# Two small opening tiles share one second stage, and the later softmax is spread over the run

## The chip, the cores and the metric

The kernel runs on one core of a Trainium2 chip. The core has five engines that run their own instruction queues: TensorE (PE, matmuls, with weight loads shown apart as PEld), VectorE (DVE), ScalarE (ACT), GpSimd (POOL) and SyncE (SP, which only issues DMAs here). The metric is the device time of one execution in microseconds; smaller is better.

## The reference

Three layers on `x` of 2 x 4160 tokens x 192 channels. Cut to what matters:

```python
# 1 attention: each token is a softmax-weighted sum of its last 7 tokens
w = softmax(weight_gen, axis=-1)                   # (2, 4160, 8 heads, 7)
out = einsum('bshk,bskhg->bshg', w, x_unf)         # 24 channels per head
# 2 first mix: a blend with the token before, then two matmuls and a gate
xk = mu_k * x + (1 - mu_k) * x_prev
xr = mu_r * x + (1 - mu_r) * x_prev
v = np.maximum(xk @ w_k, 0)**2 @ w_v               # 192 -> 1024 -> 192
x = sigmoid(xr @ w_r) * v
# 3 second mix: two matmuls with a 3-tap convolution over tokens between them
h = np.maximum(x @ w_in, 0)                        # 192 -> 1024
conv = conv_w[0]*h[t-1] + conv_w[1]*h[t] + conv_w[2]*h[t+1]
return (h * sigmoid(conv)) @ w_out                 # 1024 -> 192
```

## The kernel before

The 4160 tokens of each of the two batches are cut into ten tiles (`SIZES`: 256, 248, seven of 472, 352), and one loop runs over the tiles. The work of one tile has four parts.

`attention` runs on POOL. A tile has 2, 3 or 4 slots per batch; one slot of one batch (128 partitions, one token each) is a **token group**: a product of `rows` and `sw` (1344 elements per partition), two folding sums into `prod` and a last sum into `tok`. The weights `sw` come from `softmax`: a maximum and a subtraction, an Exp on ACT, a sum and a reciprocal on DVE, and a product on POOL. `softmax_load` 3 brings the weights of tiles 3 to 9 in one DMA.

`mixing` makes the input of the first mix. Three **flips** per tile (unit `u` 0, 2 and 1) transpose tokens on PE into a `pa` bank; ACT and DVE blend each with its shifted copy, and `hi` and `lo` split the result into two parts, `xA` for the first 128 channels and, for unit 2, `xB` for the other 64 of both batches, which DMAs put in place. Unit 2 needs all the token groups of the tile.

`moe1` is the first mix, in eight **slices** of 128 hidden channels for each batch: five matmuls into a `pa` bank (three read `xA`, two `xB`), Relu, Square and a rounded copy `s` on ACT, a remainder on DVE, and five matmuls into the banks `am` and `ar`. `gate_r` adds two gates per batch through the same two `pa` banks. `mix_out` multiplies by the gate and writes the tile `x2` of the batch.

`moe2` is the second mix, again in eight slices per batch: five matmuls from `x2` into one of two `pc` banks, then `h` (Relu), a scaled copy, two taps (`tap`, DVE), a Sigmoid, a product and the split `g`, and five matmuls into `bm` and `br`. `store` sends these out. `LAG` puts it ten steps behind `moe1`.

The weights are also split by ACT and DVE on the chip, piece by piece (`prepare`). Every call is planned at a time in steps with `at`; `Program.schedule` then takes the calls through costs of its own and writes out a fixed order for each engine. So each engine's order is settled before the run, and an instruction that waits holds up all behind it on its engine.

In the rows every call has the same line (169, after: 173), since one place issues all of them; tiles are told apart by name and width: 256 is tile 0, 248 tile 1, 472 a full tile (250, 258 and 474 where two halo columns are added).

Of the kernel before, what the change touches and what calls it, by code (L numbers as in the profile page):

```python
# [8 lines left out]
F32R = mybir.dt.float32r  # L9
# [22 lines left out]
def f(ap):  # L32
    return ap.bitcast(F32)


class Program:
# [37 lines left out]
    def cost(self, eng, method, out, ins, pointer):  # L74

        n = self.count(out)
        src = [self.space(x) for x in ins]
        if method == "dma_start":
            return 0.6, 0.0
        if eng == "PE":  # L80
            busy = max(n * 0.00045 + 0.002, 0.109)
            return busy, busy + 0.24
        if eng == "ACT":
            near = bool(src) and src[0] == "PSUM"
            p = 0.1 if pointer else 0.0
            return (0.06 if near else 0.09) + p + n / 1200, (0.2 if near else 0.24) + p + n / 1200
        if eng == "DVE":
            if method == "tensor_reduce":
                n = self.count(ins[0])
            if method == "reciprocal":  # L90
                return 0.07 + n / 160, 0.2 + n / 160
            if method in ("tensor_scalar", "tensor_copy", "memset") and "PSUM" not in src:
                return 0.07 + n / 1920, 0.2 + n / 1920
            stt = method == "scalar_tensor_tensor"
            return (0.13 if stt else 0.07) + n / 960, (0.26 if stt else 0.2) + n / 960
        if eng == "POOL":
            busy = 0.1 + (n / 455 if method == "tensor_tensor" else n / 270)
            return busy, busy + 0.12
        return 0.6, 0.6

    def schedule(self):
# [42 lines left out]
        for _ in range(n):  # L144
# [39 lines left out]
def conv_moe_kernel(ctx: ExitStack, tc: tile.TileContext, xp, wg_first, wg_rest, mus, w_k, w_v, w_r, w_in, conv_w, w_out, out):  # L184
# [210 lines left out]
    def softmax(j, a, b, eng, times, bank):  # L395
# [19 lines left out]
        for t, fn in zip(times, (lambda: fold(m, ALU.max), lambda: each(m, ALU.subtract), s3,  # L415
                                 lambda: fold(z, ALU.add), s5, lambda: each(m, ALU.mult))):
            at(t, fn)

# [35 lines left out]
    def mixing(i, u, t, dt_):  # L454
        N, P, e = SIZES[i], PART[i], EXTRA[i]
        c = 1 if u == 2 else 0
        st = {}

        def flip():
            p = pa_r()  # L460
            st["p"] = p[:, e:e + N]
            st["q"] = p
            x = tok_t[i]
            k = (0, 256, 128)[u]
            for l in range(SLOTS[i]):
                PE.transpose(p[:, l:l + SLOTS[i] * (P - 1) + 1:SLOTS[i]], x[:, l, k:k + 128], ident)

        def shifted(fn):
            a = att_r()[:, :N]
            if e:  # L470
                fn(a, st["q"][:, e - 1:e + N - 1])
            else:
                POOL.memset(a[:, 0:1], 0.0)
                fn(a[:, 1:N], st["q"][:, 0:N - 1])
            return a
# [5 lines left out]
        def m1(k):  # L481
            st[k] = (am_r, ar_r)[k]() if i == 0 else mk_r()
            col = 2 * k + c
            own = slice(col, col + 1)
            if i < 2:
                a = shifted(lambda y, x: ACT.activation(y, x, ACTF.Copy, scale=onemu[:, own]))
                DVE.scalar_tensor_tensor(out=st[k][:, :N], in0=st["p"], scalar=mu[:, own], in1=a, op0=ALU.mult, op1=ALU.add)
            else:
                DVE.scalar_tensor_tensor(out=st[k][:, :N], in0=st["d"], scalar=onemu[:, own],
                                         in1=st["p"], op0=ALU.mult, op1=ALU.add)  # L490

        def hi(k):
            if u < 2:
                x = xA_r[k]()
                xin[i, u, k, 0] = x
            else:
                x = rm_r[k]().unsqueeze(1)
            st["h", k] = x
            ACT.copy(x[:, 0, :N], st[k][:, :N])

        def lo(k):
            x = st["h", k]
            y = x[:, 1, :N] if u < 2 else (mk_r() if i == 0 else st[k])[:, :N].bitcast(F32R)
            (POOL if i else DVE).tensor_tensor(y, st[k][:, :N], f(x[:, 0, :N]), op=ALU.subtract)
            if u == 2:
                for b in range(NB):
# [5 lines left out]
                    SP.dma_start(out=f(z[oth, :N]), in_=f(y[own]))  # L512

# [249 lines left out]
    mixing(0, 1, -70, 0.1)  # L763

    for i in range(NTILE):
        T = 16 * i
        if i:
            for b in range(NB):
                attention(i, b, T - 22 + 4.5 * b, T - 15 + 4.5 * b, 1.125, POOL, (25.0 + 8 * b if i == 1 else 0.0, 0.0))
            for u, t in ((0, T - 5), (2, T - 3.7), (1, T + 3)) if i > 1 else ((0, 7), (2, 8.3), (1, 15)):  # L770
                mixing(i, u, t, 2.5)
        for b in range(NB):
# [8 lines left out]
            store(i, b, t + LAG + 10.02)  # L781

# [68 lines left out]
```

## Time and profile before

| | |
|---|---|
| median of 3 runs | 779.31 us (778.96 to 781.27) |
| time of the profiled execution | 780.29 us |
| its span, first to last instruction | 778.5 us |
| busy: PE, ACT, DVE, POOL | 694.1, 665.5, 630.8, 506.6 us |
| mean granted clock of TensorE | 0.974 |

The profiled execution's own time is 1.8 us over its span, and 1.0 us over the median. The clock is given as a share of 2.4 GHz, so 0.50 is the lower level of 1.2 GHz. Busy times of matmuls are modelled, and neighbours overlap: how fast matmuls follow each other is read from their starts.

### The profile page before, as it was taken

To read this page: it belongs to the slowest core of one execution; us is meant where nothing else is said; L and a number is where in the kernel's file an instruction comes from. 1 tells how busy PE (TensorE), PEld (TensorE's weight loads), DVE (VectorE), ACT (ScalarE), POOL (GpSimd) and SP (SyncE) were. 2 spreads that over 40 slices of the span, in tenths; PEclk is the share of its full clock that TensorE was granted. 3 is DMA by queue.
4 is the path that set the end of the run, shared out by engine and by line. 5 is a ranking of instruction groups with operands and counts; after the bars stand their busy time and mean duration, and the time that the engine had idled before them with its cause. 6 is when DMAs were issued, how large, how long until landed. Compare 5 with 4: busy or idle time off the path is not lost.

```text
span 778.5 us, 10782 instructions
## 1 busy us (share of the span) xinstructions
PE 694.1 (89%) x3505; PEld 606.3 (78%) x3505; DVE 630.8 (81%) x1137; ACT 665.5 (85%) x1441; POOL 506.6 (65%) x368
## 2 busy tenths in 40 slices
PE   0065776999999999999999999999999999999985
PEld 0054676898888888888888888888888888888974
DVE  6997977886878787878787888788788878788886
ACT  2466797998989898989998989898989899999985
POOL 6998888899999999999999798565702010110000
PEclk9996886999999999999999999999999999999999
DMA  7685010130130112111221120120002000200000
GB/s 224 197 269 180 4 52 11 58 105 11 62 101 18 53 70 51 70 51 52 69 70 51 39 78 20 45 63 7 20 0 70 1 19 1 57 0 19 19 2 28
DMA packets 19240, 45.09 MB, mean 58 GB/s; under 512 B 3056, under 2 KB 14704, under 8 KB 19056
## 3 DMA queue, kind: packets, MB, share of 16 engines
q1 hardware_dynamic: 19184, 44.41, 18.9%
q8 instruction: 27, 0.44, 0.2%
q14 instruction: 29, 0.24, 0.1%
HBM read 27.40 MB, written 6.39 MB: 43 GB/s over the span
## 4 chain that ended last, share of the span: by engine, by line
PE 68%; ACT 14%; DVE 14%; issue 2%; DMA 1%; SPq 0%; ACTq 0%; DVEq 0%
PE pa L169 21%; PE pc L169 16%; PE am L169 10%; PE bm L169 9%; PE ar L169 7%; PE br L169 6%; DVE pc L169 4%; ACT pa L169 2%; DVE stage L169 2%; ACT pc L169 2%; ACT h L169 2%; ACT g L169 2%; ACT L169 1%; DVE bm L169 1%; DVE s L169 1%
## 5 line engine op out<-in xcount | busy, mean ns | idle before, releaser
L169 DVE SCALAR_TENSOR_TENSOR pc<-h,cw,pc 128x472 f32<-128x472 f32 (+3 forms) x312 | 203.7, 653 | 34.9 <-ACT pc L169 31.9
L169 POOL TENSOR_TENSOR prod<-rows,sw 128x1344 f32<-128x1344 f32 x70 | 216.1, 3087 | 11.0 <-DMA rows<-in_x_dram 6.0
L169 ACT ACTIVATE pa<-pa 128x472 f32<-128x472 f32 (+3 forms) x324 | 162.7, 504 | 37.9 <-PE pa L169 33.8
L169 POOL TENSOR_TENSOR prod<-prod 128x576 f32<-128x576 f32 (+1 forms) x140 | 171.2, 1223 | 8.6
L169 PE MATMUL am<-s,wv 128*128 128x472 f32 (+3 forms) x480 | 146.9, 366 | 7.5 <-ACT s L169 6.0
L169 PE MATMUL bm<-g,wo 128*128 128x472 f32 (+3 forms) x465 | 144.5, 361 | 9.6 <-ACT g L169 9.0
L169 DVE TENSOR_TENSOR pc<-h,pc 128x472 f32<-128x472 f32 (+3 forms) x156 | 92.6, 594 | 54.4 <-ACT pc L169 53.0
L169 PE MATMUL pa<-xA,wkA 128*128 128x472 f32 (+3 forms) x480 | 124.4, 363 | 7.5 <-DVE s L169 3.5
L169 PE MATMUL pc<-x,wiA 128*128 128x474 f32 (+3 forms) x468 | 118.6, 361 | 3.2 <-DVE g L169 3.2
L169 POOL TENSOR_TENSOR xA<-mk,xA 128x472 fp32r<-128x472 f32 (+2 forms) x36 | 40.5, 1130 | 122.1 <-ACT xA L169 95.8
L169 PE MATMUL ar<-s,wv 128*128 128x472 f32 (+3 forms) x320 | 112.0, 362 | 5.0 <-DVE x L169 3.3
L169 PE MATMUL br<-g,wo 128*128 128x472 f32 (+3 forms) x310 | 109.4, 356 | 0.0
L169 DVE TENSOR_TENSOR s<-pa,s 128x472 fp32r<-128x472 f32 (+3 forms) x162 | 94.9, 586 | 16.0 <-ACT s L169 15.0
L169 PEld LDWEIGHTS am<-s,wv 128*128 128x128 f32 x480 | 88.7, 196 | 22.4 <-ACT s L169 11.2
L169 DVE TENSOR_TENSOR g<-pc,g 128x472 fp32r<-128x472 f32 (+3 forms) x153 | 90.4, 591 | 16.4 <-ACT g L169 14.9
L169 PEld LDWEIGHTS bm<-g,wo 128*128 128x128 f32 x465 | 86.5, 192 | 21.1 <-ACT g L169 11.5
L169 PEld LDWEIGHTS pa<-xA,wkA 128*128 128x128 f32 x480 | 86.4, 196 | 19.8 <-DVE s L169 6.3
L169 ACT ACTIVATE pc<-h,cw 128x472 f32<-128x472 f32 (+3 forms) x156 | 97.5, 625 | 1.6
L169 PEld LDWEIGHTS pc<-x,wiA 128*128 128x128 f32 x468 | 84.3, 194 | 14.0 <-DVE g L169 4.5
L169 ACT ACTIVATE h<-pc 128x474 f32<-128x474 f32 (+3 forms) x156 | 82.5, 529 | 9.6 <-PE pc L169 7.5
L169 PE MATMUL pa<-xB,wkB 128*128 128x472 f32 (+3 forms) x320 | 89.0, 359 | 1.1 <-DMA xB<-mk 1.1
L169 PE MATMUL pc<-x,wiB 128*128 128x474 f32 (+3 forms) x312 | 87.4, 359 | 0.0
(121 smaller groups left out, 1086.9 us busy)
## 6 DMA issues: line engine op xcount, KB each, us to landing
rows<-in_x_dram SPq DMA_DIRECT2D x14, 960.0 KB, 4.5
xB<-rm SPq DMA_DIRECT2D x28, 118.0 KB, 2.3
xB<-mk SPq DMA_DIRECT2D x28, 118.0 KB, 2.3
out_dram<-om SPq DMA_DIRECT2D x14, 236.0 KB, 2.0
rows<-in_x_dram SPq DMA_DIRECT2D x4, 768.0 KB, 6.6
rows<-in_x_dram SPq DMA_DIRECT2D x2, 864.0 KB, 4.3
out_dram<-ob SPq DMA_DIRECT2D x14, 118.0 KB, 2.2
stage<-in_moe_w_v_dram SPq DMA_DIRECT2D x4, 384.0 KB, 3.8
```

Of the source, the lines that this page charges most:

```text
L169: getattr(self.real[eng], method)(*a, **k)
```

## The change

- The second mix takes tiles 0 and 1 as one: `moe2` and `store` run only from tile 1 on, with 476 columns there (`UNIT`); both tiles write into the same `x2`, side by side (`OFFSET`). So there are nine second stages per batch, where there were ten.
- The tiles become 256, 220, seven of 476, and 352.
- Of the softmax of tiles 3 to 9, only the maximum and the subtraction stay close together. Tile 3 has its Exp alone; tiles 4 to 9 share one Exp over 2576 columns; the sum, the reciprocal and the last product of each tile come 16 steps apart.
- The pieces of the second mix's weights are planned at wider times. The softmax products of tiles 1 and 2 move behind the tokens of tile 0, the first `rows` load goes ahead of the first weights, and six clearings on POOL become two on DVE.
- Flips go through their slots in the other order. Unit kinds 3 and 4 are added in the code but used by no tile.
- In `schedule`: other costs for a reduction and for POOL, no delay from POOL to POOL, and `ins` no longer drops an operand that is also written.

```diff
-SIZES = [256, 248] + [472] * 7 + [352]
+SIZES = [256, 220] + [476] * 7 + [352]
+OFFSET = [0, SIZES[0]] + [0] * (NTILE - 2)
+UNIT = [None, SIZES[0] + SIZES[1]] + SIZES[2:]
...
-            busy = 0.1 + (n / 455 if method == "tensor_tensor" else n / 270)
-            return busy, busy + 0.12
+            busy = 0.15 + (n / 455 if method == "tensor_tensor" else n / 270)
+            return busy, busy + 0.1
...
-            ins = [x for x in aps if x is not out]
+            ins = [x for x in [*a[0 if "out" in k else 1:], *(v for key, v in k.items() if key != "out")]
...
-            for l in range(SLOTS[i]):
+            for l in reversed(range(SLOTS[i])):
...
-        c = slice(2, N + 2)
+        c = slice(OFFSET[i] + 2, OFFSET[i] + N + 2)
...
-        N = SIZES[i] + (2 if last else 0)
+        N = UNIT[i] + (2 if last else 0)
...
-        softmax(3, a, b, POOL, (16.5 + 0.3 * j, 16.6 + 0.3 * j, 19.5 + 0.1 * j, 20.5 + 0.5 * j, 20.6 + 0.5 * j, 24.9 + 16 * j), None)
+        softmax(3, a, b, POOL, (30.3, 30.4, 31.2, 32.0, 32.1, 34.9) if j == 0 else
+                (36.9 + 1.2 * j, 37 + 1.2 * j, None, 30 + 16 * j, 30.1 + 16 * j, 32.5 + 16 * j), None)
+    a = slots[3]
+    at(45.3, lambda: ACT.activation(sm[3][0][:, a:], sm[3][0][:, a:], ACTF.Exp))
...
-                moe2(i, b, fi, t + fi + LAG)
+                if i:
+                    moe2(i, b, fi, t + fi + LAG)
```

How the orders move, at three places.

POOL, before, among the token groups of tile 2 (`tok_79`; `sw<-sw,stage` are steps of the softmax of tiles 3 to 9):

```order
TENSOR_TENSOR prod<-prod 128x384
TENSOR_TENSOR sw<-sw,stage 128x448 x2
TENSOR_TENSOR tok_79<-prod 128x192
TENSOR_TENSOR sw<-sw,stage 128x448 x4
TENSOR_TENSOR sw<-sw,stage 128x336
TENSOR_TENSOR prod<-rows_76,sw 128x1344
TENSOR_TENSOR sw<-sw,stage 128x448
```

POOL, after, from the last token group of tile 2 on:

```order
TENSOR_TENSOR prod<-rows_77,sw 128x1344
TENSOR_TENSOR prod<-prod 128x576
TENSOR_TENSOR prod<-prod 128x384
TENSOR_TENSOR tok_79<-prod 128x192
TENSOR_TENSOR xA_87<-mk_83,xA_87 128x476
TENSOR_TENSOR xA_89<-mk_84,xA_89 128x476
TENSOR_TENSOR sw<-sw,stage 128x448 x2
TENSOR_TENSOR mk_83<-mk_83,rm_85 128x476
TENSOR_TENSOR sw<-sw,stage 128x448 x2
TENSOR_TENSOR mk_84<-mk_84,rm_86 128x476
TENSOR_TENSOR sw<-sw,stage 128x448
```

All fourteen such steps stood ahead of tile 2's last token group; now none does, and five stand between it and tile 3's first.

ACT, before, at one of the Exps of the later softmax (there are seven, among slices of the first two tiles):

```order
ACTIVATE pa_111<-pa_111 128x256 x2
ACT_TABLE_LOAD
ACTIVATE sw<-sw 128x448
ACT_TABLE_LOAD
ACTIVATE pc_113<-pc_113 128x256
```

ACT, after, at the one Exp of tiles 4 to 9, which stands among slices of tile 2:

```order
ACTIVATE h_103<-pc_113 128x478
ACT_TABLE_LOAD
ACTIVATE sw<-sw 128x2576
ACTIVATE pc_113<-h_103,cw 128x476
ACTIVATE pa_111<-pa_111 128x476
CAST rm_85<-mk_83 128x476
ACT_TABLE_LOAD
ACTIVATE r_97<-pa_112 128x476
```

Fourteen table loads become six: two early ones, two around tile 3's Exp and these two.

PE, before, where the first matmul of tile 2 stands (`pa_111<-xA_87,wkA`, 472 wide); `pc` rows are second stages of tile 1:

```order
MATMUL pc_113<-x_0_73,wiA 128x250 x3
MATMUL pc_113<-x_0_73,wiB 128x250 x2
MATMUL bm<-g_101,wo 128x248 x2
MATMUL br<-g_101,wo 128x248
MATMUL bm<-g_101,wo 128x248
MATMUL br<-g_101,wo 128x248
MATMUL am<-s_99,wv 128x248 x2
MATMUL ar<-s_99,wv 128x248
MATMUL pa_111<-xA_87,wkA 128x472
```

PE, after, at the same place, from the flip of tile 2's unit 2 on:

```order
MATMUL pa_111<-ident,tok_79 128x128 x4
MATMUL pc_114<-x_0_73,wiA 128x478 x3
MATMUL pc_114<-x_0_73,wiB 128x478 x2
MATMUL bm<-g_102,wo 128x476
MATMUL br<-g_102,wo 128x476
MATMUL am<-s_100,wv 128x220 x2
MATMUL ar<-s_100,wv 128x220
MATMUL am<-s_100,wv 128x220
MATMUL ar<-s_100,wv 128x220
MATMUL pa_112<-xA_87,wkA 128x476 x3
```

Before, all 16 slices of tile 0's second stage and five of tile 1's stand ahead of this matmul; now six of the joint second stage do, and ten are left.

## Rows read from the trace of the kernel before

**Rows 1.** The page: span, and busy time (share) and instructions by engine
```profile
span 778.5 us, 10782 instructions
PE 694.1 (89%) x3505; PEld 606.3 (78%) x3505; DVE 630.8 (81%) x1137; ACT 665.5 (85%) x1441; POOL 506.6 (65%) x368
```

**Rows 2.** Stretches: busy us (x instructions) by engine, granted clock, DMA
```profile
40.00:60.00 20.00, 13.96 (x75) 12.00 (x75) 18.04 (x40) 14.96 (x43) 19.05 (x16) 1.00 0.90 268
...
66.00:82.00 16.00, 9.91 (x41) 9.06 (x42) 14.94 (x34) 10.28 (x29) 15.53 (x12) 0.50 0.24 65
...
82.00:94.00 12.00, 8.87 (x63) 7.52 (x61) 11.59 (x23) 10.71 (x26) 9.10 (x10) 1.00 0.00 1
...
240.00:680.00 440.00, 437.37 (x2060) 377.95 (x2059) 357.58 (x579) 400.34 (x801) 290.56 (x200) 1.00 0.14 43
```

**Rows 3.** Timeline of PE, where tile 2 begins: start us, us, instruction
```profile
40.27 0.98 PE L169 MATMUL pa<-xA,wkA 128*128 128x256 f32 x3 [2.33 <-ACT rm L169]
...
150.89 0.52 PE L169 MATMUL pc<-x,wiA 128*128 128x250 f32 x3
...
152.07 0.40 PE L169 MATMUL pa<-xA,wkA 128*128 128x248 f32 x2
...
154.55 0.63 PE L169 MATMUL pa<-ident,tok 128*128 128x128 f32 x4 [1.17 <-DVE mk L169]
...
163.36 0.72 PE L169 MATMUL pa<-xA,wkA 128*128 128x472 f32 x4
...
246.51 0.81 PE L169 MATMUL pc<-x,wiA 128*128 128x474 f32 x3
...
248.64 0.58 PE L169 MATMUL am<-s,wv 128*128 128x472 f32 x2
```

**Rows 4.** Timeline of POOL: one token group and the next, tile 2's last
```profile
43.62 3.04 POOL L169 TENSOR_TENSOR prod<-rows,sw 128x1344 f32<-128x1344 f32 x1
...
49.98 3.06 POOL L169 TENSOR_TENSOR prod<-rows,sw 128x1344 f32<-128x1344 f32 x1
...
139.14 0.59 POOL L169 TENSOR_TENSOR tok<-prod 128x192 f32<-128x192 f32 x1
```

**Rows 5.** A POOL group in 40:140 us: busy, mean ns, idle before
```profile
L169 POOL TENSOR_TENSOR sw<-sw,stage 128x448 f32<-128x448 f32 (+1 forms) x14 | 15.3, 1106 | 5.8 <-DVE stage L169 3.6 <-ACT h L169 2.2
```

**Rows 6.** Timeline of ACT: first and last of twelve table loads
```profile
88.97 1.28 ACT L169 ACT_TABLE_LOAD   x1
...
90.26 0.58 ACT L169 ACTIVATE sw<-sw 128x448 f32<-128x448 f32 x1
...
128.02 1.28 ACT L169 ACT_TABLE_LOAD   x1
```

**Rows 7.** Timeline of PE: a wait that follows such a pair of loads
```profile
95.89 0.80 PE L169 MATMUL bm<-g,wo 128*128 128x256 f32 x2 [2.30 <-ACT g L169]
```

**Rows 8.** Groups with shapes kept apart, second stage and table loads: ACT
```profile
L169 ACT ACT_TABLE_LOAD x14 | 18.0, 1283 | 3.8 <-DMA sw<-in_first_dram 3.6
...
L169 ACT ACTIVATE pc<-pc 128x472 f32<-128x472 f32 x112 | 61.8, 552 | 2.9 <-DVE pc L169 2.3
...
L169 ACT ACTIVATE pc<-pc 128x256 f32<-128x256 f32 x16 | 5.9, 372 | 0.1
...
L169 ACT ACTIVATE pc<-h,cw 128x472 f32<-128x472 f32 x112 | 75.1, 670 | 1.1
...
L169 ACT ACTIVATE pc<-h,cw 128x256 f32<-128x256 f32 x16 | 7.8, 486 | 0.1
```

**Rows 9.** Groups with shapes kept apart, second stage and a softmax sum: DVE
```profile
L169 DVE SCALAR_TENSOR_TENSOR pc<-h,cw,pc 128x472 f32<-128x472 f32 x224 | 159.0, 710 | 28.1 <-ACT pc L169 25.9
...
L169 DVE SCALAR_TENSOR_TENSOR pc<-h,cw,pc 128x256 f32<-128x256 f32 x32 | 15.4, 480 | 2.4 <-ACT pc L169 2.3
...
L169 DVE TENSOR_TENSOR pc<-h,pc 128x256 f32<-128x256 f32 x16 | 6.7, 418 | 3.2 <-ACT pc L169 3.0
...
L169 DVE TENSOR_REDUCE stage<-sw 128x64 f32<-128x448 f32 x12 | 11.6, 987 | 5.5 <-ACT sw L169 5.5
```

More of the change, by code (lines that the diff above doesn't have):

```diff
@@ L109, in schedule @@
             out = k["out"] if "out" in k else aps[0]
-            ins = [x for x in aps if x is not out]
+            ins = [x for x in [*a[0 if "out" in k else 1:], *(v for key, v in k.items() if key != "out")]
+                   if hasattr(x, "tensor") and hasattr(x, "ap")]
             dur[i], late[i] = self.cost(eng, method, out, ins, any(x is not None and x in ("scale",) and hasattr(k[x], "tensor") for x in k))
@@ L162, in schedule @@
             for j in succ[i]:
-                ready[j] = max(ready[j], t + dur[i] if eng == "PE" == self.ops[j][0] else end)
+                ready[j] = max(ready[j], t + dur[i] if eng in ("PE", "POOL") and eng == self.ops[j][0] else end)
                 left[j] -= 1
@@ L416, in softmax @@
                                  lambda: fold(z, ALU.add), s5, lambda: each(m, ALU.mult))):
-            at(t, fn)
+            if t is not None:
+                at(t, fn)
     rows_t, tok_t = {}, {}
@@ L455, in mixing @@
         N, P, e = SIZES[i], PART[i], EXTRA[i]
-        c = 1 if u == 2 else 0
+        c = 1 if u >= 2 else 0
+        O = slice(64 if u == 4 else 0, 64 if u == 3 else 128)
         st = {}
@@ L460, in flip @@
             p = pa_r()
-            st["p"] = p[:, e:e + N]
+            st["p"] = p[O, e:e + N]
             st["q"] = p
             x = tok_t[i]
-            k = (0, 256, 128)[u]
-            for l in range(SLOTS[i]):
-                PE.transpose(p[:, l:l + SLOTS[i] * (P - 1) + 1:SLOTS[i]], x[:, l, k:k + 128], ident)
+            k, n = ((0, 128), (256, 128), (128, 128), (128, 64), (128, 128))[u]
+            for l in reversed(range(SLOTS[i])):
+                PE.transpose(p[0:n, l:l + SLOTS[i] * (P - 1) + 1:SLOTS[i]], x[:, l, k:k + n], ident)
         def shifted(fn):
-            a = att_r()[:, :N]
+            a = att_r()[O, :N]
             if e:
-                fn(a, st["q"][:, e - 1:e + N - 1])
+                fn(a, st["q"][O, e - 1:e + N - 1])
             else:
-                POOL.memset(a[:, 0:1], 0.0)
-                fn(a[:, 1:N], st["q"][:, 0:N - 1])
+                fn(a[:, 1:N], st["q"][O, 0:N - 1])
             return a
@@ L481, in m1 @@
         def m1(k):
-            st[k] = (am_r, ar_r)[k]() if i == 0 else mk_r()
+            st[k] = ar_r.tiles[0][:, 256 * k:256 * k + 256] if i == 0 else mk_r()
             col = 2 * k + c
@@ L485, in m1 @@
             if i < 2:
-                a = shifted(lambda y, x: ACT.activation(y, x, ACTF.Copy, scale=onemu[:, own]))
-                DVE.scalar_tensor_tensor(out=st[k][:, :N], in0=st["p"], scalar=mu[:, own], in1=a, op0=ALU.mult, op1=ALU.add)
+                a = shifted(lambda y, x: ACT.activation(y, x, ACTF.Copy, scale=onemu[O, own]))
+                DVE.scalar_tensor_tensor(out=st[k][O, :N], in0=st["p"], scalar=mu[O, own], in1=a, op0=ALU.mult, op1=ALU.add)
             else:
-                DVE.scalar_tensor_tensor(out=st[k][:, :N], in0=st["d"], scalar=onemu[:, own],
+                DVE.scalar_tensor_tensor(out=st[k][O, :N], in0=st["d"], scalar=onemu[O, own],
                                          in1=st["p"], op0=ALU.mult, op1=ALU.add)
@@ L498, in hi @@
             st["h", k] = x
-            ACT.copy(x[:, 0, :N], st[k][:, :N])
+            ACT.copy(x[O, 0, :N], st[k][O, :N])
         def lo(k):
             x = st["h", k]
[L503 to L506, printed above, removed]
+            y = x[O, 1, :N] if u < 2 else (mk_r() if i == 0 else st[k])[O, :N].bitcast(F32R)
+            (POOL if i else DVE).tensor_tensor(y, st[k][O, :N], f(x[O, 0, :N]), op=ALU.subtract)
+            if u >= 2:
+                for b in range(NB) if u == 2 else (u - 3,):
                     z = xB_r[k]()
@@ L511, in lo @@
                     SP.dma_start(out=f(z[own, :N]), in_=f(x[own, 0, :N]))
-                    SP.dma_start(out=f(z[oth, :N]), in_=f(y[own]))
+                    SP.dma_start(out=f(z[oth, :N]), in_=f(y[own] if u == 2 else y))
         at(t, flip)
@@ L602, in go @@
                 POOL.memset(f(x2[b][:, :, 0:2]), 0.0)
-            else:
-                n = SIZES[i - 1]
+            elif i > 1:
+                n = UNIT[i - 1]
                 ACT.copy(x2[b][:, :, 0:2], f(x2[b][:, :, n:n + 2]))
@@ L626, in a1 @@
         def a1():
+            ACT.copy(X[0:64, 3, c], r[0:64, :N])
             ACT.copy(X[:, 2, c], r[:, :N])
-            ACT.copy(X[0:64, 3, c], r[0:64, :N])
         def d2():
@@ L705, in store @@
     def store(i, b, t):
-        N = SIZES[i]
+        N = UNIT[i]
         last = i == NTILE - 1
-        a = 1 if i == 0 else 0
+        a = 1 if i == 1 else 0
         n = N + (1 if last else 0)
-        t0 = STARTS[i] - 1
+        t0 = STARTS[i] - OFFSET[i] - 1
         st = {}
@@ L739, in identity, with before_first @@
                            pattern=[[-1, 128]], channel_multiplier=1)
+    def before_first():
+        for a in att_r.tiles:
+            DVE.memset(a[:, 0:1], 0.0)
     at(-101, identity)
-    at(-100.5, consts)
+    at(-100.9, before_first)
+    at(-99.8, consts)
     softmax_load(0, wg_first, -100)
     softmax(0, 0, slots[0], DVE, (-95, -94.9, -94.8, -94.7, -94.6, -94.5), am_r.tiles[0])
-    attention(0, 0, -99.9, -90, 0.1, POOL)
+    attention(0, 0, -100.1, -90, 0.1, POOL)
     attention(0, 1, -99.6, -83.7, 0.1, POOL)
     softmax_load(1, wg_rest[:, :slots[1] * KH], -99.5)
-    softmax(1, 0, slots[1], POOL, (-82.6, -82.5, -82.4, -82.35, -82.3, -82.25), ar_r.tiles[0])
+    softmax(1, 0, slots[1], POOL, (-83.85, -83.65, -83.64, -83.63, -83.62, -83.55), am_r.tiles[0])
     prepare((-99.75, -99.7, -99.4), [(-82, chunk_rem(w_k, wkB, True)), (-81, chunk_in(w_k, wkA, 0)),
@@ L763, in conv_moe_kernel @@
     mixing(0, 1, -70, 0.1)
+    UNITS = {1: ((0, 7), (2, 8.3), (1, 15))}
     for i in range(NTILE):
@@ L768, in conv_moe_kernel @@
             for b in range(NB):
-                attention(i, b, T - 22 + 4.5 * b, T - 15 + 4.5 * b, 1.125, POOL, (25.0 + 8 * b if i == 1 else 0.0, 0.0))
-            for u, t in ((0, T - 5), (2, T - 3.7), (1, T + 3)) if i > 1 else ((0, 7), (2, 8.3), (1, 15)):
+                attention(i, b, T - 22 + 4.5 * b, T - 15 + 4.5 * b + (2 if i == 3 else 0), 1.125, POOL, (25.0 + 8 * b if i == 1 else 0.0, 0.0))
+            for u, t in UNITS.get(i, ((0, T - 5), (2, T - 3.7), (1, T + 3))):
                 mixing(i, u, t, 2.5)
```

13 lines of the change are left out of this document (7 added, 6 removed).

## The prediction

> **What bounds the kernel now.** The page first: PE is busy longest, 694 of 778.5 us [rows 1]. A table of stretches then says where that holds. From 240 to 680 us PE is busy 437.4 of 440 us at the full clock [rows 2]: there PE alone sets the pace, and nothing on ACT, DVE or POOL matters that stays within it. Before that it doesn't hold. In 40 to 60 us PE is busy 14.0 of 20 us beside DVE's 18.0 and POOL's 19.1, and in 66 to 82 us 9.9 of 16, at a granted clock of 0.50, the lower level of 1.2 GHz [rows 2]. The timelines name the stages: the first matmul of tile 0 is at 40.27 us, the first of tile 2 at 163.36 us [rows 3]. In these 123 us PE does little more than the first mix of two small tiles, the second mix of one and a third of the other's.
>
> So I price the change at one point, the first matmul of tile 2: how much work it leaves to PE behind that point, and how much earlier the point comes. Before, 778.5 - 163.4 = 615.1 us follow it, nearly all paced by PE, and I take their waits and the tail over as they are.
>
> **What it leaves behind the point.** A slice of the second mix is ten matmuls. At 474 columns they take 248.64 - 246.51 = 2.13 us, at 250 152.07 - 150.89 = 1.18 us [rows 3]. Before, 11 of tile 1's 16 slices are left: 13.0 us. Now 10 of the joint 16, at 2.13 x 476/472 = 2.15: 21.5 us, so +8.5. Two slices in either order still owe their output matmuls: +1.0 (two times half of 2.15 less half of 1.18). The seven full tiles have 4 more columns in each of 340 matmuls, 0.213 us x 4/472 x 340 = 0.61 us each: +4.3. Together +13.8 us. The total of columns hardly changes; it only lies more behind the point. If tile 2 did not begin before 163.4 - 13.8 = 149.6 us, nothing would be won.
>
> **When tile 2 begins now: three chains.**
>
> POOL makes the tokens. Tile 2's last token group ends at 139.14 + 0.59 = 139.7 us [rows 4]. Of the time until there, the 14 steps of the later softmax took 15.3 us, and POOL stood idle 5.8 us in front of them, for DVE and ACT [rows 5]. All of them now come later, so 139.7 - 21.1 = 118.6 us. In-order waits can eat some of it: six subtractions for tile 1's `xA` and `mk` now stand between groups, each behind ACT's `hi`. None to 10 us, I take 1.5, as POOL comes to them when ACT has mostly done them: 120 us. Behind the last token came the flip, the blend, the split and the DMAs of `xB`: 163.36 - 154.55 = 8.8 us [rows 3]. With a microsecond for the flip's place in PE's queue, tile 2 begins at about 130 us.
>
> ACT. A second-mix slice at 256 columns costs 0.486 + 3 x 0.372 = 1.60 us (the Sigmoid's row stands for `h` and `g` too), at 472 0.670 + 3 x 0.552 = 2.33 [rows 8]. Ahead of the point stood 21 small slices, 33.6 us; now six large, 14.0: -19.6. Twelve of 14 table loads lay between 88.97 and 128.02 us [rows 6], of which two remain there: 10 x 1.283 = -12.8 [rows 8]. Six Exps of 0.58 go too [rows 6]: -3.5. Together -36 us, so not later than POOL: 163.4 - 36 = 127.
>
> DVE. A slice is two taps and two products: 2 x 0.480 + 2 x 0.418 = 1.80 us at 256; at 472 2 x 0.710 + 2 x 0.65, the 0.65 being my estimate with the taps' slope [rows 9]. 21 x 1.80 = 37.8 becomes 6 x 2.72 = 16.3: -21.5. The softmax sums of six tiles go behind the point, 6 x 0.99 = -5.9 [rows 9], their reciprocals as well, unpriced. So at the latest 163.4 - 27.4 = 136.
>
> The latest is between 130 and 136, and a chain that is worked out as if its engine never rested is a bound, not a time. I take 131 us, near POOL's; 126 with no waits on POOL, 138 with DVE's bound and some waits.
>
> **What comes back later.** The one Exp falls among slices of tile 2, where PE has no slack. Its length is 0.58 + (2576 - 448) x (0.552 - 0.372)/216 = 2.35 us [rows 6, 8], with two table loads 4.9 us during which ACT serves nothing else, though three other calls stand inside. A pair of loads around a 0.58 us Exp, 3.1 us, left PE idle 2.30 us [rows 7]. So 0 if slices are ahead, up to 2.3 + 1.8 = 4.1; ACT is busy 400 of 440 us in the stretch that PE paces [rows 2] and can't have much ahead: 3 us. The Trainium skill ("ScalarE: Activation LUTs", "What ACT_TABLE_LOAD costs") puts a drain of about 1.38 us on top of the load's 1.283; the trace agrees on the load, while the Exp starts 1.29 us after the load does, with no such gap. By the page the two loads would make 2.8 us more, a median of about 768, still inside the forecast's own range.
>
> Then tile 3's tokens. POOL has about ten other steps of 1.1 us, eight groups of 6.36 us (49.98 - 43.62) [rows 4] and, say, 6 us of waits and later steps after 120: 187 us. In the new order 275 matmuls of 0.215 us stand between tile 2's first matmul and the flip that needs these tokens: 131 + 59 = 190. The cover is only 3 us; I put 1 us for it. From tile 4 on POOL is ahead. The six sums and reciprocals now fall where DVE is busy 358 of 440 us [rows 2], which covers some 2 us per 75; without that cover each would cost PE up to 2 us.
>
> The rest I price at nothing: the reversed flips have as many transposes, the first `rows` load goes ahead of two small ones, and DVE bounds the opening as well, and the wider spread of weight pieces moves DVE work within a stretch already counted. If the pieces became late, the joint second mix would wait for them, and tile 2 with it.
>
> **Sum.** 131 + 615.1 + 13.8 + 3 + 1 = 763.9 us of span. The profiled execution's own time is 1.8 us over its span and 1.0 over the median, so about 765 as a median, against 779.3.
>
> **Rivals.**
> *PE falls to its lower clock in the new opening (slower).* For a while only the first mix runs, so PE rests more. In 66 to 82 us the clock was 0.50 and 41 matmuls took 16 us, 0.39 each; at 1.00, in 82 to 94 us, 63 took 12, 0.19 each [rows 2]. The new order has 420 matmuls before tile 2. My 131 us mean 0.217 each from 40 us on; 149.6 us mean 0.26, which is reached when 35% run at the slow pace. If half did, 0.29 each: tile 2 at 162, the end at 796. For it: in the old opening too PE slowed as soon as others held it up. Against: a slow matmul only counts where PE, not POOL, is last. 9%. The Trainium skill ("TensorE: Matmul & The Clock Gate", "What's actually happening") calls the throttled clock the default, from which a busy engine is released; the trace agrees, 0.50 where PE waits and 1.00 where it is fed.
>
> *The opening isn't shortened (no change).* Two `pa` banks carry slices, gates and flips, and with the second mix gone PE waits for ACT and DVE at every bank. 48 uses (32 slices, 8 gates, 8 flips) at 1.33 us, the pace of 75 matmuls in 20 us [rows 2], are 64 us from 40 us on, well within; it takes 2.3 us each to reach 149.6. Time then 777 to 782. 6%.
>
> *Tile 3's tokens late, the Exp in full.* POOL waits 8 us more: 5 us on PE, and 1 for the Exp: 772 to 777. 10%.
>
> *More is won.* No waits on POOL, a cheap Exp: 752 to 757. 9%.
>
> **How the numbers follow.** The forecast, 757 to 772, has 66%; 765 is its value. The range takes it with the late tokens and a little of the better case: 756 to 777. A difference under 0.3%, 2.3 us, can hardly be told from none. Faster: 66 + 10 + 9 = 85%; within 0.3%: 6%; slower: 9%.
>
> **What would show it.** After: tile 2's last token on POOL near 120 us, no `sw` steps ahead of it; tile 2's first matmul between 126 and 138; six table loads; one Exp of about 2.35 us, with a wait of 2 to 4 us on PE behind it; a full tile's period some 0.6 us longer; no wait of PE for POOL at tile 3 above 3 us. Wrong would be: tile 2's start after 145 us, a clock of 0.5 over much of 60 to 120 us, or repeated waits for POOL after 200 us.

## The result, and the profile after

The changed kernel takes 770.15 us (769.84 to 771.47), the kernel before 779.33: a ratio of 0.988, 95% interval 0.9861 to 0.9900. The profiled execution has 771.47 us and a span of 769.7. So 8.8 us of span are gone where I forecast 14.6; the time lies in the range, 5 us above its value.

The page first: its span, its row of PE and other engines, and the chain that ended last, by engine.

```profile
span 769.7 us, 10269 instructions
...
PE 692.0 (90%) x3345; PEld 589.8 (77%) x3345; DVE 625.5 (81%) x1073; ACT 648.2 (84%) x1358; POOL 506.3 (66%) x362
...
PE 43%; POOL 39%; ACT 6%; issue 4%; DVE 4%; DMA 2%; SPq 0%; ACTq 0%; POOLq 0%
```

PE does 2.1 us less than in [rows 1]. POOL is busy no longer than before, yet 39% of the last chain is POOL's; the chain of before (PE 68%, ACT 14%, DVE 14%) has no POOL in it.

The stretches of [rows 2] now:

```profile
40.00:60.00 20.00, 14.45 (x70) 13.27 (x70) 17.18 (x35) 12.28 (x35) 18.09 (x14) 1.00 0.61 192
66.00:82.00 16.00, 13.30 (x80) 11.82 (x80) 10.78 (x24) 11.56 (x33) 14.30 (x14) 0.79 0.51 153
82.00:94.00 12.00, 8.92 (x61) 7.51 (x62) 11.54 (x29) 9.73 (x34) 9.14 (x8) 1.00 0.01 2
240.00:680.00 440.00, 434.80 (x2027) 372.19 (x2026) 355.42 (x572) 395.38 (x786) 292.37 (x202) 1.00 0.15 42
```

In 66 to 82 us PE does twice the matmuls of [rows 2]. In 240 to 680 us it now rests 5.2 us, where it rested 2.6. PE's timeline shows the places; the first three rows answer to [rows 3]:

```profile
40.08 0.98 PE L173 MATMUL pa<-xA,wkA 128*128 128x256 f32 x3 [2.04 <-DVE ar L173]
...
124.58 0.65 PE L173 MATMUL pa<-ident,tok 128*128 128x128 f32 x4 [0.94 <-POOL tok L173]
...
127.13 0.82 PE L173 MATMUL pa<-xA,wkA 128*128 128x476 f32 x3
...
189.95 1.11 PE L173 MATMUL pa<-ident,tok 128*128 128x128 f32 x4 [1.99 <-POOL tok L173]
...
212.18 0.92 PE L173 MATMUL pc<-x,wiA 128*128 128x478 f32 x3 [0.73 <-DVE g L173]
...
356.17 0.92 PE L173 MATMUL pa<-xA,wrA 128*128 128x476 f32 x3 [1.39 <-DVE mk L173]
...
434.55 0.91 PE L173 MATMUL pa<-xA,wrA 128*128 128x476 f32 x3 [2.45 <-DVE mk L173]
```

Tile 2 begins at 127.1 us, 36.2 earlier than in [rows 3]. The interval between the first transposes of one tile and the next, in us, shows what was given back (75.5 is a tile of 476 columns that waits for next to nothing, 75.2 one of 472; each interval has the same 352 matmuls):

| | tile 3 at | 3 to 4 | 4 to 5 | 5 to 6 | 6 to 7 | 7 to 8 |
|---|---|---|---|---|---|---|
| before | 206.4 | 76.1 | 75.2 | 75.2 | 75.2 | 75.2 |
| after | 181.5 | 85.1 | 75.5 | 77.3 | 79.8 | 75.6 |

Of 24.9 us at tile 3, 16.3 are given back by tile 8: 1.5 because the tiles are wider, the rest at tile 3 (9.6, before 0.9) and at tiles 5 and 6 (1.8 and 4.3). Not all of that is waiting. The stretches of the intervals of tiles 3, 4 and 6 (each also counts a matmul or two that run over its ends):

```profile
181.51:266.64 85.13, 79.17 (x353) 65.12 (x352) 73.99 (x118) 74.33 (x141) 77.76 (x55) 0.98 0.19 56
266.64:342.18 75.54, 75.26 (x354) 64.58 (x352) 61.90 (x100) 69.12 (x138) 72.56 (x51) 1.00 0.20 62
419.50:499.26 79.76, 77.05 (x353) 65.66 (x352) 61.95 (x100) 69.07 (x137) 70.62 (x49) 0.98 0.18 57
```

PE rests 5.96 us at tile 3 and 2.71 at tile 6, against 0.28 at tile 4. Part of the rest is PE's clock: it was 0.67 in 190 to 195 us, behind the wait for tile 3's tokens, and fell again behind the wait at tile 6. The prediction had looked for that in the opening alone.

Two rows of DVE and four of POOL say what the wait at tile 6 is for:

```profile
429.12 0.65 DVE L173 TENSOR_TENSOR g<-pc,g 128x476 fp32r<-128x476 f32 x1
432.55 0.71 DVE L173 SCALAR_TENSOR_TENSOR mk<-att,onemu,pa 128x476 f32<-128x476 f32 x1 [2.79 <-POOL xA L173]
```
```profile
426.45 0.60 POOL L173 TENSOR_TENSOR tok<-prod 128x192 f32<-128x192 f32 x1
427.01 1.16 POOL L173 TENSOR_TENSOR sw<-sw,stage 128x448 f32<-128x448 f32 x1
428.25 3.10 POOL L173 TENSOR_TENSOR prod<-rows,sw 128x1344 f32<-128x1344 f32 x1
431.31 2.35 POOL L173 TENSOR_TENSOR xA<-mk,xA 128x476 fp32r<-128x476 f32 x2
```

PE waits for the `pa` bank of tile 6's second flip, which is free when DVE has blended it into `mk`, a ring of two. Both buffers of `mk` hold the first flip's blend (DVE wrote them at 421.6 and 423.4) until POOL has made its low part, `xA<-mk`. POOL has no idle time here. It has just made tile 7's last token, which is not flipped before 505.1 us, and its order puts two steps for tile 8 ahead of the split. Behind the wait PE has work to the end.

### The profile page after: what moved, and what is told of

Its sections match the earlier page's. It is cut to its first block, busy times and chain, and to the rows that moved or that the text cites. A ratio compares the mean times of both kernels' runs of the same rounds, so it can differ in the third digit from the quotient of the medians.

```text
span 769.7 us, 10269 instructions
## 1 busy us (share of the span) xinstructions
PE 692.0 (90%) x3345; PEld 589.8 (77%) x3345; DVE 625.5 (81%) x1073; ACT 648.2 (84%) x1358; POOL 506.3 (66%) x362
## 4 chain that ended last, share of the span: by engine, by line
PE 43%; POOL 39%; ACT 6%; issue 4%; DVE 4%; DMA 2%; SPq 0%; ACTq 0%; POOLq 0%
POOL prod L173 32%; PE pa L173 14%; PE pc L173 10%; PE am L173 6%; PE bm L173 6%; PE ar L173 4%; PE br L173 4%; POOL tok L173 4%; POOL xA L173 2%; ACT pa L173 1%; ACT pc L173 1%; DVE pc L173 1%; DMA wkB<-x 1%; POOL sw L173 1%; DMA xB<-mk 1%
## 5 line engine op out<-in xcount | busy, mean ns | idle before, releaser
L173 DVE SCALAR_TENSOR_TENSOR pc<-h,cw,pc 128x476 f32<-128x476 f32 (+1 forms) x280 | 196.7, 703 | 30.3 <-ACT pc L173 27.7
L173 ACT ACTIVATE pa<-pa 128x476 f32<-128x476 f32 (+3 forms) x324 | 162.5, 503 | 43.6 <-PE pa L173 39.5
L173 PE MATMUL am<-s,wv 128*128 128x476 f32 (+3 forms) x480 | 148.7, 367 | 10.2 <-ACT s L173 6.1
L173 PE MATMUL bm<-g,wo 128*128 128x476 f32 (+1 forms) x417 | 138.8, 381 | 6.3 <-ACT g L173 5.9
L173 PE MATMUL pa<-xA,wkA 128*128 128x476 f32 (+3 forms) x480 | 123.6, 365 | 8.2 <-DVE ar L173 5.4
L173 PE MATMUL pc<-x,wiA 128*128 128x478 f32 (+1 forms) x420 | 116.2, 378 | 1.4 <-DVE g L173 1.2
L173 PE MATMUL ar<-s,wv 128*128 128x476 f32 (+3 forms) x320 | 111.5, 358 | 0.0
L173 DVE TENSOR_TENSOR s<-pa,s 128x476 fp32r<-128x476 f32 (+3 forms) x162 | 94.6, 586 | 18.4 <-ACT s L173 17.6
L173 PE MATMUL br<-g,wo 128*128 128x476 f32 (+1 forms) x278 | 104.5, 376 | 0.0
L173 ACT ACTIVATE pc<-h,cw 128x476 f32<-128x476 f32 (+1 forms) x140 | 92.5, 660 | 1.5
L173 ACT ACTIVATE h<-pc 128x478 f32<-128x478 f32 (+1 forms) x140 | 79.8, 570 | 14.9 <-PE pc L173 11.9
L173 PEld LDWEIGHTS pc<-x,wiA 128*128 128x128 f32 x420 | 76.1, 188 | 14.5 <-DVE g L173 3.6
```

The costliest lines, as they stand in the source:

```text
L173: getattr(self.real[eng], method)(*a, **k)
```

## The experiments

Each kernel was timed beside the kernel before, which had 779.5 to 779.9 us; ratios are to that. Theory 1: POOL's queue is the last link, as I first put it up to tile 3. Theory 2: ACT with the wide Exp. Theory 3: the gain is the joint mix's alone. Theories 4 and 5 came up on the way: POOL is late by its order (4) or by its amount of work (5). All edits but those of e4 and e5b go through the planner, which then moves other steps as well.

**e1: old load order.**
```diff
-    at(-99.8, consts)
+    at(-100.5, consts)
-    attention(0, 0, -100.1, -90, 0.1, POOL)
+    attention(0, 0, -99.9, -90, 0.1, POOL)
```


> The order of the first loads on SP's queue is put back to that of the kernel before: the first tile's softmax weights and the mixing constants are issued ahead of the first 768 KB of rows. Nothing else changes. Theory 1 (GpSimd, POOL in the profile, is the last link up to tile 3's mixing): the first product on POOL starts at about 7.4 us in place of 11.15, the last tokens of tiles 2 and 3 come about 3.7 us earlier (120.8 and 186.2 in place of 124.5 and 189.9), and the end is 2 to 4 us earlier: 766 to 768. Theory 2 (ACT, with the wide Exp in the stage that TensorE paces, sets the end): the opening moves, but the end stays within 1 us of 770.

Measured 766.54 us, ratio 0.9838 (0.9823 to 0.9852): 3.6 us less than the changed kernel. POOL's first product, of the changed kernel and of this one:

```profile
11.15 3.02 POOL L173 TENSOR_TENSOR prod<-rows,sw 128x1344 f32<-128x1344 f32 x1 [9.80 <-DVE sw L173]
```
```profile
6.84 3.02 POOL L173 TENSOR_TENSOR prod<-rows,sw 128x1344 f32<-128x1344 f32 x1 [5.49 <-DVE sw L173]
```

4.3 us earlier at the first step, 4.9 at the splits of tile 6 (the second ends at 428.7 in place of 433.7), 4.8 at the end of the span. Only 1.75 of the 4.3 us are the load: DVE first reads the weights at 3.38 us in place of 5.13. The rest is DVE's order, in which the changed kernel has three steps of weight splitting, and a wait of 1.04 us for ACT, among those of this softmax. Theory 1 holds here, and theory 2 by itself falls.

**e4: no wide Exp.**
```diff
             eng, method, a, k = self.ops[i][:4]
+            if method == "activation" and self.count(a[0]) > 2000:
+                continue
```


> The one Exp of 2576 values for tiles 4 to 9 is left out, in the order that the planner gives with it, so these tiles use weights that were not exponentiated; its two table loads go as well. Theory 2 (the wide Exp behind tile 3's tokens gave part of the gain back): PE's waits between 190 and 215 us, near 7 us with those for tile 3's tokens, shrink, and the end is 3 to 5 us earlier (765 to 767). Theory 1 (tile 3's tokens are late on POOL, and the Exp lies largely beside that and other waits): at most 2 us earlier (768 to 770).

Measured 768.01 us, 0.9856 (0.9843 to 0.9868): 2.1 us less, at the edge of theory 1. The changed kernel's ACT and POOL show the path:

```profile
192.45 0.60 ACT L173 ACTIVATE h<-pc 128x478 f32<-128x478 f32 x1
193.07 1.28 ACT L173 ACT_TABLE_LOAD   x1
194.36 2.36 ACT L173 ACTIVATE sw<-sw 128x2576 f32<-128x2576 f32 x1
...
197.65 0.58 ACT L173 CAST rm<-mk 128x476 fp32r<-128x476 f32 x1
```
```profile
198.31 1.28 POOL L173 TENSOR_TENSOR mk<-mk,rm 128x476 fp32r<-128x476 f32 x1 [4.11 <-ACT rm L173]
```

The high part `rm` of tile 3 stands behind the Exp on ACT, and POOL waits 4.11 us for it with its queue of tokens behind. Without the Exp that wait is 1.43 us, and the splits of tile 6 end 2.0 us earlier. The profiled execution's span is 3.5 us shorter, though (that of the changed kernel is 1.3 us above its median): the other 1.5 us come behind the wait at tile 6, which is hardly longer (2.60 us for 2.45). The ten microseconds from its end on, in the changed kernel and in this one:

```profile
434.55:444.55 10.00, 10.00 (x39) 8.50 (x40) 5.93 (x10) 7.94 (x16) 9.69 (x8) 0.83 0.39 90
432.55:442.55 10.00, 10.00 (x46) 8.50 (x47) 7.10 (x11) 9.11 (x19) 9.69 (x8) 1.00 0.39 89
```

Seven matmuls fewer at a clock of 0.83 are 1.5 us at the full clock's 0.21 us each. In 190 to 195 us too the clock is 1.00 here, so that the 2.0 us need not be the Exp's alone. What makes the clock fall behind one such wait and not behind another, no run shows.

**e2: seven Exps again.**
```diff
-    softmax_load(3, ..., 18.2, 50.0)
+    softmax_load(3, ..., 18.2, 40.0)
-        softmax(3, a, b, POOL, (30.3, ...) if j == 0 else (36.9 + 1.2 * j, ...), None)
-    at(45.3, lambda: ACT.activation(sm[3][0][:, a:], sm[3][0][:, a:], ACTF.Exp))
+        softmax(3, a, b, POOL, (18.5 + 0.3 * j, 18.6 + 0.3 * j, 21.5 + 0.1 * j, 22.5 + 0.5 * j,
+                                22.6 + 0.5 * j, 24.9 + 16 * j), None)
```


> The later softmax is put back to seven Exps in a row near the time that the kernel before had them (its load is released earlier to match); the joint second mix and all else stay as in the changed kernel. Theory 1 (POOL's order up to tile 2's tokens carries the gain): the softmax products and subtractions come back ahead of tile 2's tokens, these end about 15 us later (138 to 142 in place of 124.5), and the time goes up by 6 to 10 us, to 776 to 780. Theory 3 (the joint mix carries the gain): the time stays within 2 us of 770. Theory 2 (the wide Exp gave some of the gain back): 2 to 4 us less than Theory 1 says, as tile 3's mixing has no wide Exp behind it.

Measured 774.72 us, 0.9934 (0.9919 to 0.9948): 4.6 us more. The time lies under theory 1's 776 to 780, within what theory 2 leaves of it (772 to 778). Tile 2's tokens end at 132.5, only 8 us later, PE's granted clock is 0.57 in 82 to 94 us, and tile 3 begins at 194.3, 12.8 later. But behind it the intervals lose 3.6 us where the changed kernel's lose 15.8: what the spread softmax wins ahead of tile 3 it largely gives back. Of the six executions the profiled one is the shortest (772.16 us, 0.7 over the changed kernel's profiled one); the others have lower mean clocks, 0.969 to 0.971 for its 0.975, but no trace shows where. By the median theory 3 falls.

**e7: old times of the weight pieces, and e3b: those and no joint mix.**
```diff
-                (6.0, chunk_rem(w_in, ...)), (8.0, ...), (10.0, ...), (10.4, ...), (12.0, ...), (14.0, ...), (16.0, ...), (18.0, ...)
+                (4.4, chunk_rem(w_in, ...)), (5.0, ...), (6.0, ...), (6.4, ...), (7.0, ...), (8.0, ...), (9.0, ...), (10.0, ...)
```


> The pieces of the second mix's weights are prepared at the times of the kernel before (4.4 to 10.0 in place of 6.0 to 18.0), with the joint second mix kept. Expected by the prediction's step (priced at nothing): within 1.5 us of 770. Rival: bunched pieces hold up DVE and ACT in the first mixes of tiles 0 and 1, tile 2 begins 3 to 8 us later, and the end is 2 to 6 us later (772 to 776).

Measured 775.53 us, 0.9936 (0.9920 to 0.9953): 5.4 us more, the rival. Tile 2's tokens are as early (124.4), but its first matmul is at 134.9, for PE is the late one:

```profile
66.00:82.00 16.00, 11.03 (x57) 9.88 (x56) 10.80 (x24) 10.14 (x29) 15.21 (x15) 0.71 0.50 160
82.00:94.00 12.00, 8.50 (x48) 7.28 (x47) 10.40 (x25) 7.95 (x27) 8.71 (x7) 0.78 0.00 1
94.00:110.00 16.00, 14.27 (x93) 13.58 (x94) 8.92 (x18) 8.16 (x28) 15.22 (x11) 0.81 0.18 63
```

57 and 48 matmuls where the changed kernel has 80 and 61, at a granted clock of 0.71 to 0.81 where it has 0.79 and then 1.00.

e3b has these times too, and the joint mix undone:
```diff
-OFFSET = [0, SIZES[0]] + [0] * (NTILE - 2)
-UNIT = [None, SIZES[0] + SIZES[1]] + SIZES[2:]
+OFFSET = [0] * NTILE
+UNIT = SIZES
...
-                if i:
-                    moe2(i, b, fi, t + fi + LAG)
+                moe2(i, b, fi, t + fi + LAG)
```


> The joint second mix is undone: tile 0 has its own eight slices of 256 columns for each of both batch halves and its own store, tile 1 its own of 220, and the pieces of the second mix's weights are prepared at the times of the kernel before, since tile 0's own second mix needs them that early. The spread softmax, the load order, the sizes and the reversed flips stay as in the changed kernel. Theory 1: POOL's order is unchanged, so the last tokens of tile 2 stay within 4 us of 124.5; TensorE, VectorE and ACT do the added slices while tile 2's tokens are waited for, and the time goes up by 0 to 5 us (770 to 775). Theory 3 (the joint mix carries the gain, since ACT or VectorE with their added slices end later than POOL): tile 2's first matmul falls back to 138 or later and the time goes back to 777 to 780.

Measured 778.91 us, 1.0001 (0.9992 to 1.0010): the kernel before. Tile 2's tokens stay at 122.6, as theory 1 says, yet its first matmul is at 145.6, and with the time that is what theory 3 forecast. It isn't the joint mix alone, for the pieces are in this edit too, and by e7 they make up 5.4 of its 8.8 us. So theory 1 missed: in the opening two chains are nearly level, and the joint mix and the later pieces free the one through PE, ACT and DVE, the later softmax POOL's. Against e7 the joint mix itself is 3.4 us by the medians, 1.3 by the profiled executions.

**g1: POOL dearer in the planner, and g0: cheaper.** g1's edit; g0 has 0.10:
```diff
-            busy = 0.15 + (n / 455 if method == "tensor_tensor" else n / 270)
+            busy = 0.23 + (n / 455 if method == "tensor_tensor" else n / 270)
```


> One number in the planner: the fixed part of a POOL step is 0.23 us in place of 0.15 (a token's four steps take 6.45 us in the trace, 6.08 by the planner). The work is the same; of POOL's order only the splits of the mixed tokens (xA, mk) change place: in tiles 4 to 6 they stand one to three product steps earlier. Theory 4 (the waits at tiles 5 and 6 come from POOL's order, in which work for later tiles stands ahead of the split that PE needs): the intervals between the first flips of tiles 5, 6 and 7, now 77.3 and 79.8 us, fall to 75.6, and the end is 4 to 6 us earlier, 764 to 766. Rival, theory 5 (POOL has too much work up to there, in any order): other steps come late instead, and the end stays within 1.5 us of 770.

> The mirror of the planner's 0.23 us: the fixed part of a POOL step is 0.10 us, as the kernel before had it (the change made it 0.15). The splits of tiles 4 and 5 stand one or two product steps further back on POOL, those of tile 6 where they were. Theory 4 (that order sets the waits): the waits of tiles 4 to 6 grow by some 3 to 7 us in all, 773 to 777. Theory 5 (only the amount of work on POOL counts): within 1.5 us of 770.

g1 measured 764.72 us, 0.9799 (0.9782 to 0.9816): 5.4 us less. The intervals from tile 3 on are 80.3, 75.5, 75.6, 75.5. POOL's busy time is 0.8 us more. Its split at tile 6 now stands ahead of the token's last steps, and the chain is PE's again:

```profile
421.28 1.22 POOL L173 TENSOR_TENSOR xA<-mk,xA 128x476 fp32r<-128x476 f32 x1
422.46 1.01 POOL L173 TENSOR_TENSOR prod<-prod 128x384 f32<-128x384 f32 x1
```
```profile
PE 73%; ACT 10%; DVE 7%; POOL 5%; issue 2%; DMA 1%; SPq 0%; ACTq 0%; POOLq 0%; DVEq 0%
```

g0 measured 773.45 us, 0.9915 (0.9901 to 0.9929): 3.3 us more; its wait at tile 5 is

```profile
360.44 1.56 PE L173 MATMUL pa<-xA,wrA 128*128 128x476 f32 x3 [5.26 <-DVE mk L173]
```

and that interval 83.0. From about 250 us on the orders of PE, ACT and DVE in g0 and g1 are the changed kernel's, and only POOL's differs where these waits stand. Theory 4 holds: POOL's order sets them. The 0.05 us that the change itself put on a POOL step was part of the gain.

**g2: the product later.**
```diff
-                (36.9 + 1.2 * j, 37 + 1.2 * j, None, 30 + 16 * j, 30.1 + 16 * j, 32.5 + 16 * j), None)
+                (36.9 + 1.2 * j, 37 + 1.2 * j, None, 30 + 16 * j, 30.1 + 16 * j, 36.5 + 16 * j), None)
```


> The softmax product of each later tile is placed a quarter of a tile later (36.5 + 16 j for 32.5 + 16 j), so that it stands behind the splits of tile 6 and not ahead of them; nothing else changes. Theory 4: DVE's wait for the split at tile 6 falls by the product's 1.16 us there, and the end is about 1 us earlier (768.5 to 769.5). If the product were the main cause of that wait, 2.5 to 4 us earlier (766 to 767.5).

In this kernel the tokens of the first batch element are made before the product, so with weights not divided by their sum. Measured 771.07 us, 0.9886 (0.9868 to 0.9904), as the changed kernel; the interval at tile 6 is 80.2. A miss for both: the product's 1.16 us are gone from there, but the planner put the last three steps of a token, 3.0 us, ahead of or between the two splits, which end at 433.1 in place of 433.7.

**e5: no maximum; e5b: the same in the old order.** e5 plans without these steps, e5b drops them from the changed kernel's finished order:
```diff
-        for t, fn in zip(times, (lambda: fold(m, ALU.max), lambda: each(m, ALU.subtract), s3,
+        for t, fn in zip(times, (lambda: None, lambda: None, s3,
```


> Every softmax leaves out its maximum and the subtraction of it (the same result but for rounding, as the inputs are small). That takes one step of 0.65 to 1.17 us from POOL per tile from tile 1 on, two of them ahead of tile 2's last token and five more ahead of tile 3's, and one sum-like step of about 1 us per tile from DVE. Theory 1 (POOL is the last link, in the opening and again wherever its queue is behind PE): tile 2's tokens come about 1.8 us earlier, tile 3's about 7 us, the waits near 356 and 434 us go, and the end is 6 to 11 us earlier, 759 to 764. Theory 2 (TensorE's own work and the wide Exp set what is left): the end moves by no more than 2 us, 768 to 770.

> The order of the changed kernel is kept word for word, and the maximum and the subtraction of every softmax are then left out of it (the same result but for rounding), so that no planner puts other work in their place. Theory 1 with theory 4 (POOL's queue is late wherever it is waited for, and a shorter queue brings all that stands in it forward): tile 2's tokens about 3 us earlier, tile 3's about 8, the splits of tiles 5 and 6 about 9; the waits of 1.39 and 2.45 us there go, and the end is 7 to 11 us earlier, 759 to 763. Rival, theory 2 (TensorE, DVE and ACT hold what is left, as the 767.5 of the run with a new plan suggests): 765 to 768.

e5 measured 767.48 us, 0.9818 (0.9792 to 0.9845), e5b 766.94, 0.9835 (0.9817 to 0.9853): 2.7 and 3.2 us less, both far under what theory 1 said; e5b lies in its rival's 765 to 768, e5 in neither range. e5's new plan put the splits behind more tokens again (5 to 6: 80.2). In e5b POOL's timeline shows where the time went:

```profile
126.40 1.21 POOL L175 TENSOR_TENSOR mk<-mk,rm 128x476 fp32r<-128x476 f32 x1 [1.79 <-ACT rm L175]
130.43 1.21 POOL L175 TENSOR_TENSOR mk<-mk,rm 128x476 fp32r<-128x476 f32 x1 [2.83 <-ACT rm L175]
...
194.63 1.25 POOL L175 TENSOR_TENSOR mk<-mk,rm 128x476 fp32r<-128x476 f32 x1 [5.61 <-ACT rm L175]
```

Four subtractions behind tile 2's tokens had filled the waits for `rm`, the second of which stands behind tile 3's small Exp on ACT. Taken away, 4.5 us of work leave 4.6 of waits, where 0.27 were. The wait behind the wide Exp grows from 4.11 to 5.61 us. The splits of tile 6 end 3.7 us earlier and not 9, and the clock does not fall behind the wait there.

**e6: flips in rising order.**
```diff
-            for l in reversed(range(SLOTS[i])):
+            for l in range(SLOTS[i]):
```


> The transposes of a flip take the slots in the old, rising order. Expected by the prediction's step (priced at nothing): within 1 us of 770. Rival: the reversed order lets the flip start later or earlier on the last token, since the last slot's token comes last; then, with the last token taken last again, the flips of tiles 2 and 3 wait less, and the end is 0.5 to 1.5 us earlier (768.6 to 769.6).

Measured 767.75 us, 0.9838 (0.9825 to 0.9851): 2.4 us less, past the rival's 1.5. At tile 3, where the changed kernel does all four transposes behind the last token, only one is left:

```profile
185.57 0.49 PE L173 MATMUL pa<-ident,tok 128*128 128x128 f32 x3
188.14 0.33 PE L173 MATMUL pa<-ident,tok 128*128 128x128 f32 x1 [1.44 <-POOL tok L173]
```

POOL's tokens of tiles 2 and 3 also come 1.5 and 1.8 us earlier here, though POOL's order is the changed kernel's until behind tile 6. Two of its waits in the opening are gone, these of the changed kernel:

```profile
44.09 1.14 POOL L173 TENSOR_TENSOR sw<-sw,smz 128x448 f32<-128x448 f32 x1 [1.04 <-DVE smz L173]
71.53 1.26 POOL L173 TENSOR_TENSOR mk<-mk,rm 128x220 fp32r<-128x220 f32 x2 [1.27 <-ACT rm L173]
```

The first product starts 0.4 us later in e6, and the wait behind the wide Exp is 3.30 us in place of 4.11. So the gain reaches POOL as shorter waits for DVE and ACT; how the flips' order shortens them is open.

**g3: e1 and g1 together.**

> The old order of the first loads together with the planner's 0.23 us for POOL. Theories 1 and 4 hold at different places (the opening; tiles 5 and 6), so the gains add: 3.6 us and 4 to 6 us, 761 to 763. If the one only moves the other's wait (theory 5): 765 to 767.

Measured 761.03 us (759.69 to 761.62), 0.9752 (0.9733 to 0.9770): the gains add, 9.1 us under the changed kernel and the fastest of all. Its long stretch:

```profile
240.00:680.00 440.00, 438.63 (x2059) 376.70 (x2059) 360.69 (x581) 401.61 (x802) 297.00 (x206) 1.00 0.15 42
```

Forward flips with both were not tried.

**What ties them together.** From the end of the wait at tile 6 to the end of the span it is 335.1 us in the changed kernel and g2, 335.3 in e1, 335.2 in e6, 333.6 in e4, 333.7 in e5b, 336.4 in e7. The spread is PE's clock in the ten us behind that wait of 2.45 to 2.86 us: 0.83 in the first four, 1.00 in e4 and e5b, 0.69 in e7. So with that order the end is POOL's split at tile 6 plus 335 us, less or more 1.5 by the clock, and an edit is worth what it moves that split.

## Why the prediction was right, and where it failed

**Tile 2's start: right within 4 us, by a bound that was level with another.** Forecast 131, measured 127.1. POOL's tokens ended at 124.5, not 120: 3.8 of these 4.5 us are the first product, 11.15 for 7.34. The step from the last token to the first matmul took 2.6 us and not 9.8, as the first flip was long done (106.3 us). PE's clock, a rival, was 0.79 in 66 to 82 us and 1.00 from 82 us on; e2 and e7, with 0.57 to 0.82 up to 110 us, show how near that rival was.

**Work behind the point: right.** The period grew by 0.3 to 0.4 us where I had 0.6; PE's busy time in all fell by 2.1.

**"What comes back later" is the step that failed.** I had 3 + 1 us; the intervals lost 15.8 us from tile 3 to tile 7 against 1.0 before. From 127.1 us to the end it took 642.5 us where my sum has 632.9. Three parts:
- "From tile 4 on POOL is ahead" is true of tokens and wrong of the splits in the same queue: 6.1 us at tiles 5 and 6. g1 takes them away by order alone. I had counted when POOL's product is needed, not what stands ahead of the small steps that PE needs. Of the 4.3 us at tile 6 about 1.5 are the lower clock behind the wait, for which my sum has no term this late.
- The Exp: forecast 3; without it (e4) the splits of tile 6 end 2.0 us earlier, with some of that perhaps the clock's. Not PE's next slice paid for it, but POOL's wait for `rm`. The Trainium skill ("ScalarE: Activation LUTs", "What ACT_TABLE_LOAD costs") puts a drain of about 1.38 us on top of the load. Here the load starts 0.02 us behind the end of the step before it and the Exp 1.29 us after the load starts, so the 2.8 us more that the page would have made did not come.
- Tile 3: 1 us forecast. The wait for its tokens was 1.99, the whole interval 9.6 too long, of which PE rests 5.7 more than at tile 4; 3.9 of its waits stand behind steps of ACT and DVE. g1 brings it to 4.8 too long, though there tile 3 begins 4.1 us later. In 206 to 241 us the changed kernel's DVE is busy 34.66 of 35 us; the later tiles' sums and reciprocals are not spread over them but bunched there, 9.6 us in these groups, so the "cover" that I gave them was missing:

```profile
L173 DVE TENSOR_SCALAR stage<-stage 128x64 f32<-128x64 f32 x3 | 3.6, 1199 | 0.0
L173 DVE TENSOR_REDUCE stage<-sw 128x64 f32<-128x448 f32 x3 | 3.0, 995 | 0.0
L173 DVE RECIPROCAL stage<-stage 128x64 f32<-128x64 f32 x4 | 2.2, 544 | 0.0
...
L173 DVE TENSOR_REDUCE stage<-sw 128x48 f32<-128x336 f32 x1 | 0.8, 818 | 0.0
```

How tile 3's 9.6 us divide between tokens, clock, order and DVE is open.

**"The rest I price at nothing" failed three times.** Load order: 3.6 us lost (e1), part of it by the DVE steps that the planner then put among the first softmax; the reason that I gave, that DVE bounds the opening as well, did not hold. Reversed flips: 2.4 lost (e6). Spread of the weight pieces: 5.4 won (e7). They nearly cancel, so the value of 765 owes something to luck; in e3b, without pieces and joint mix, nothing is left of the gain.

**The rivals.** Tile 3's tokens late was the nearest in mechanism, at a smaller price; my sign that would show the forecast wrong, repeated waits for POOL after 200 us, came true.

## What to carry to other kernels

An engine with slack in its main product can still be last: look in its queue for the small steps that others wait for, and for what stands ahead of them. When a stage is shortened, check the order further back, for it was planned for the old pace. And before a busy step is priced as a gain, see what wait it fills: 7.5 us taken off POOL ahead of tile 3 gave 3. A wait on PE can also cost more than its length: behind 2.45 us at tile 6 came 1.5 us at a lower clock.

## What the hardware showed besides

A DVE step on 64 values per partition, SBUF to SBUF (`stage<-stage`, adding a constant), took 0.20 us at best and 2.26 at worst:

```profile
209.30 2.26 DVE L173 TENSOR_SCALAR stage<-stage 128x64 f32<-128x64 f32 x1
211.49 0.64 DVE L173 TENSOR_TENSOR g<-pc,g 128x476 fp32r<-128x476 f32 x1
```
```profile
208.44 3.07 POOL L173 TENSOR_TENSOR prod<-rows,sw 128x1344 f32<-128x1344 f32 x1
```

It ends at 211.56, POOL's running product at 211.51. That is no chance: in the traces of all kernels here 25 of these steps took over 1 us, and every one ends 0.04 to 0.06 us behind the end of the POOL step that was running when it started. So the slow ones wait until POOL's step is done, though the two work on different tiles of SBUF; by what means, no run here shows. PE's wait of 0.73 us at 212.18 is for the `g` behind it. And a small load issued at 1.17 us, 0.4 us behind one of 768 KB, was first read at 5.13 us; in e1, issued at 1.18 us ahead of that one, at 3.38.
